# One order for all steps of a retention and SwiGLU kernel is replaced by another

## The chip, the cores and the metric

The kernel runs on one core of a Trainium2 chip (trn2). The time is that of one execution on the device in microseconds (us), the median of several executions.

## The reference

A retention layer (a linear attention with a decay per head) feeds a SwiGLU feed-forward block. All data is fp32.

```python
batch, n_heads, seq, head_dim = (4, 8, 768, 64)
for t in range(S):
    state = gamma * state + k_t (outer) v_t          # one 64 x 64 state per batch and head
    y[:, :, t] = scale * (q_t @ state)
x = y as (3072 tokens, 512)
g = x @ w_gate                                       # 512 x 1536
out = (g * sigmoid(g) * (x @ w_val)) @ w_out         # 1536 x 512
```

## The kernel before

**The work.** The 3072 tokens are cut into four segments of 768 tokens, numbered 0 to 3. A segment is six chunks of 128 tokens: three pairs (p = 0, 1, 2), the two of a pair from two batches. A segment has three stages: attention (its output y becomes the input x of the block), up (12 tiles f of the hidden width, gate and value), and down (12 tiles f, six token groups per tile). fp32 accuracy comes from three terms: each matrix is split into three parts, and every product is three matmul passes a = 0, 1, 2 over these parts. The three parts of an operand are made by three steps on three engines in turn: ScalarE (part 0), VectorE or GpSimd (part 1), GpSimd or VectorE (part 2).

**Stages in time.** Segment 0 loads the weights from the inputs in raw form, converts them and stores them in DRAM for the later segments. The attention of segment s+1 runs inside the down stage of segment s: its small matmuls stand between the down matmuls. So the order in time is: attention of segment 0 (the head), up 0, down 0 with attention 1, up 1, down 1 with attention 2, up 2, down 2 with attention 3, up 3, down 3. The up stages of segments 1 to 3 use seven products instead of eight (`up3`), which needs sums of x and of the weights.

**The order.** Each step is a small function with a key. `PLAN` is one string with all 2371 keys. `run()` walks it and calls each step; a call issues all instructions of the step, each on its engine or DMA queue. Every engine, and the SyncE queue that issues nearly all DMAs, executes in the order of issue. So `PLAN` fixes the order on each of them. Semaphores between engines are set by the framework from what each instruction reads and writes. Buffers of the splits rotate (four `gitem`, three `oitem`), and the PSUM banks are named in the code.

```python
    def run():
        for key in PLAN.split():
            if key in events:
                events.pop(key)[2]()
            else:
                do(key)
```

**Keys of segment 0.** `ln:w` loads chunk n (w = 0 k turned, 1 q turned, 2 v, 3 k by rows; DMA L472). The q of chunks 0 and 1 are loaded on ScalarE's queue ahead of `PLAN`. `A0 A1 A2` load the table of decays in three parts (two masks, and the rest; L594). `U`, `V` load raw weights (L519). `sn` is the scores of chunk n (PE L636, then two VectorE multiplications by the masks, L642), `kn`/`Kn` the scaled keys (GpSimd or VectorE L657), `tn` the state (PE L692), `on` the part of the old state (PE L707), `mn` the output (PE L721, then ScalarE L977), `xn:1`, `xn:2` the other two parts of x. `a b S c C` convert raw weights, `T` makes sums of weights in the buffer `first` (VectorE L407), `Z` stores these to DRAM (L490). `n` splits weights, `p`, `v` (PE L914) and `G`, `W` (PE L896) are the gate and value products.

**Keys with a segment, `s/...`.** `D f.tok` are three down matmuls (PE L1128). `h f.0` to `h f.2` split the hidden tile (ScalarE L968, VectorE L971, VectorE L407); `d f.0` to `d f.2` split `w_out` in segment 0 (ScalarE L977, GpSimd L980, VectorE L984); `W f` loads it. Attention of pair p: `sc p` the scores, `A p`, `B p`, `C p` the three groups of PE passes (all PE L766, 64x64 matmuls), `dec`, `q`, `k` the scalings, `was p.z` the decayed state (ScalarE L865), `new p.z` two adds of the new state out of PSUM (VectorE L871), `y p.z j` eight copies of y out of PSUM (ScalarE L999) for each half z, `sum`, `x` the sums and splits of x. Banks 6 and 7 hold all that `A`, `B` and `C` write, and `new` and `y` read. `w`, `p`, `u` are weights, products and the SwiGLU arithmetic of `up3`, `L` loads a tile of up weights, `e` writes out.

**One buffer twice.** `first` (segment 0: chunk 5's q and k, three sums of weights, one raw w_out tile) and `xb` (a part of x from segment 1 on) have the same place in SBUF. The first write to `xb` is `1/x0.2.0` on ScalarE; the last store out of `first` is `Z10`.

Of the kernel before, what the change touches and what calls it, by code (L numbers as in the profile page):

```python
# [25 lines left out]
L = 3  # L26
# [30 lines left out]
    p1:1 x5:2 Z0 u1:1 T1:2 c12 v1:0 U5:1 y1:0 v1:1 p0:2 Z1 l5:3 v0:2 c2 C2 b12 y1:1 p1:2 n2:0 a4
    U6:0 u0:2 b3 n2:1 u1:2 v1:2 S12 n2:3 L y0:2 S3 c3 n2:2 U13:2 G2:0 i2:0 n2:4 y1:2 C3 g4 T2:0
    b4 T2:1 n3:0 C12 n2:5 G2:1 i2:1 a5 T2:2 n3:1 Z2 n3:2 S4 n3:3 n3:4 c4 T3:0 C4 W2:0 j2:0 T3:1
    W2:1 G3:1 U7:1 c13 T3:2 G3:0 n4:0 Z12 n3:5 n4:1 i3:1 W3:0 Z3 n4:2 b5 a6 j2:1 i3:0 S5 n4:3  # L60
    G4:1 n4:4 c5 W3:1 T4:0 h2 U8:0 C5 T4:1 T4:2 n4:5 G4:0 a13 i4:1 n5:0 j3:0 n5:1 n5:3 n5:2 b6
    U14:3 i4:0 a7 W4:0 n5:4 j3:1 G5:1 S6 c6 b13 Z4 j4:0 T5:0 T5:1 C6 W4:1 n6:0 U9:1 T5:2 n5:5 b7
    a8 S13 W5:0 G5:0 j4:1 c14 Z5 W5:1 i5:0 i5:1 n6:1 S7 j5:1 n6:3 n6:4 c7 a9 C7 n7:0 n6:2 G6:0
    U10:0 j5:0 b8 G6:1 T6:0 n7:1 n7:3 S8 C13 T6:1 i6:1 i6:0 n6:5 n7:2 c8 Z13 l4:3 a14 n7:4 b14
    W6:1 W6:0 T6:2 C8 T7:0 S14 U15:2 n7:5 n8:0 j6:0 G7:1 j6:1 i7:1 U11:1 C14 b9 G7:0 n8:3 W7:1
    S9 n8:1 c15 n8:2 W7:0 c9 Z6 i7:0 j7:1 a10 P1 C9 n8:4 G8:1 n8:5 T7:1 j7:0 n9:0 b10 Z14 k4
    U16:3 g5 T7:2 S10 T8:0 G8:0 n9:1 a15 b15 P2 c10 Z7 W8:0 T8:1 n9:2 S15 T8:2 Z8 W8:1 C15 C10
    n9:3 i8:1 i8:0 k5 G9:1 Z15 a11 b11 j8:0 j8:1 n10:0 n9:4 S11 n9:5 t4 U17:2 c16 n10:1 G9:0
    T9:0 i9:0 t5 n10:3 n10:2 W9:1 a16 b16 n10:4 n10:5 S16 W9:0 T9:1 j9:0 P0 i9:1 c11 0/h0.0
    G10:0 G10:1 C11 n11:0 j9:1 W10:1 n11:3 i10:0 C16 Z16 i10:1 T9:2 n11:4 Z9 T11:0 T11:1 n11:5  # L70
    a17 b17 T11:2 W10:0 n11:1 T10:0 Z11 0/h0.1 S17 T10:1 j10:0 0/W0 c17 0/h1.0 n11:2 h1 G11:0
    C17 j10:1 i11:0 0/d0.0 G11:1 1/sc0 1/dec0.0 0/W1 1/l3 1/l5 1/q0.0 i11:1 0/h2.0 0/d0.1 0/h0.2
    0/h4.0 0/d1.0 W11:0 0/d0.2 1/k0.0 W11:1 1/l4 j11:0 0/D0.0 0/D0.2 1/dec0.1 0/d1.1 j11:1
# [14 lines left out]
    1/sc2 0/D6.3 1/sum1.2 0/D7.2 1/x1.2.1 1/sum1.1 0/h9.1 1/dec2.0 0/D7.4 0/Z7 1/q2.0 0/D7.0  # L88
    1/q2.1 0/D7.5 0/h10.0 1/dec2.1 0/d8.0 0/h10.1 0/W9 1/k2.0 0/D7.3 1/k2.1 1/sum1.3 1/x1.0.0
    0/D7.1 1/A2 0/d8.1 0/d8.2 0/d9.0 1/L0 1/x1.1.2 1/x1.1.1 1/new2.0 0/D8.4 0/d9.1 0/h11.0  # L90
    0/D8.2 0/h9.2 0/d9.2 0/D8.1 0/D8.0 1/x1.2.2 0/D8.5 0/W10 0/h11.1 0/h11.2 0/Z8 0/d10.0
    0/d10.1 0/D9.4 1/B2 0/d10.2 0/D8.3 1/y2.00 0/h10.2 1/w0.0.0 1/y2.01 1/y2.06 0/W11 1/y2.02
    0/D9.0 1/w0.0.1 0/D9.1 1/y2.07 0/D9.2 0/D9.3 1/y2.03 1/y2.04 1/y2.05 1/C2 0/D9.5 1/y2.16
    0/D10.0 1/y2.15 1/L1 1/x1.0.1 0/D10.3 0/Z9 1/y2.11 0/D10.1 1/x1.0.2 1/w0.0.2 1/y2.14 0/d11.0
    1/y2.17 0/D10.2 1/y2.13 1/sum2.0 1/y2.10 0/d11.1 0/d11.2 1/y2.12 0/Z10 0/D10.4 1/x2.1.0
    0/D10.5 1/sum2.1 1/w0.1.0 1/sum2.3 1/L2 0/D11.3 1/sum2.2 0/D11.4 0/D11.1 1/x2.0.0 1/x2.1.2
    0/D11.0 1/w1.0.0 0/D11.2 1/x2.1.1 1/x2.0.1 0/D11.5 1/x2.2.0 1/w1.0.1 0/e0 1/p0.0 0/Z11
    1/x2.0.2 1/u0.0 1/w1.0.2 1/p0.1 1/p0.2 1/u0.1 1/x2.2.1 1/p1.0 1/p1.1 0/e2 1/w0.1.1 1/w0.2.0
# [1205 lines left out]
```

## Time and profile before

| | |
|---|---|
| median of 3 executions | 648.29 us (647.54 to 648.67) |
| the profiled execution | 652.34 us |
| span of its instructions | 650.5 us |
| PE busy | 635.7 us |
| VectorE busy | 489.6 us |
| ScalarE busy | 392.4 us |
| GpSimd busy | 272.3 us |
| moved by DMA | 140.13 MB |

A profile row gives the start of an instruction or a merged group, its length, engine, source line, operation, output and inputs, shape and count; in brackets stands how long the engine was idle before, and what ended that. PE is TensorE's matmul part, PEld its weight load, DVE VectorE, ACT ScalarE, POOL GpSimd, SPq the queue of SyncE. PEclk is the share of the full TensorE clock that was granted. An fp32 matmul of 64 rows, and any other that isn't split by hand, shows as two.

### The profile page before, as it was taken

The page shows a single profiled execution, that of the slowest core. Times are in us where ns is not written, and L with a number is a line of the kernel's source. Part 1 is how long each engine was busy: PE and PEld are TensorE (multiplying, and loading weights), DVE is VectorE, ACT ScalarE, POOL GpSimd, SP SyncE. Part 2 cuts the span into 40 slices and gives each one's busy share as a digit, 9 for nine tenths or more (in the row PEclk, how much of TensorE's full clock was granted, in tenths as well). Part 3 has the DMA queues.
Part 4 walks back from the last instruction along what each step waited for, and adds up shares of the span by engine and source line. Part 5 has one row for each costly group of instructions (what it writes and reads, how often), then busy time and mean ns, then how long its engine had stood idle before and what let it go on. Part 6 is the DMA issues. An engine that isn't in the chain of part 4 may idle for free.

```text
span 650.5 us, 14090 instructions
## 1 busy us (share of the span) xinstructions
PE 635.7 (98%) x5576; PEld 581.5 (89%) x5576; DVE 489.6 (75%) x712; ACT 392.4 (60%) x860; POOL 272.3 (42%) x174
## 2 busy tenths in 40 slices
...
GB/s 323 374 356 332 350 327 278 198 361 261 300 183 313 152 146 171 36 245 248 247 215 209 235 116 65 123 194 286 115 260 270 156 188 141 133 11 158 177 215 147
DMA packets 50050, 140.13 MB, mean 215 GB/s; under 512 B 4928, under 2 KB 17472, under 8 KB 49984
## 3 DMA queue, kind: packets, MB, share of 16 engines
...
## 4 chain that ended last, share of the span: by engine, by line
PE 89%; DMA 4%; DVE 3%; ACT 2%; issue 1%; SPq 0%; ACTq 0%; DVEq 0%
PE bank L1065 40%; PE bank L1128 27%; PE bank L896 13%; PE bank L766 5%; PE bank L914 2%; DMA rawp<-in_w_gate_dram 1%; ACT chunk_x L999 1%; DMA hT<-in_k_n_dram 1%; DMA hT<-in_q_t_dram 1%; DVE oitem L984 0%; DMA loads<-in_v_n_dram 0%; DVE xb L407 0%; PE bank L721 0%; ACT states L865 0%; DVE tmp L407 0%
## 5 line engine op out<-in xcount | busy, mean ns | idle before, releaser
L1128 PE MATMUL bank<-oitem,gitem 128*128 128x512 f32 x864 | 210.9, 398 | 5.6 <-DVE oitem L984 2.9
L1128 PEld LDWEIGHTS bank<-oitem,gitem 128*128 128x128 f32 x864 | 160.5, 189 | 41.8 <-DVE oitem L984 4.4
L974 POOL TENSOR_TENSOR gitem<-gitem 128x768 fp32r<-128x768 f32 x72 | 143.7, 2005 | 100.7 <-DVE gitem L971 74.2
L1065 PE MATMUL bank<-xa,gitem 128*128 128x384 f32 x864 | 160.7, 334 | 0.0
L1065 PEld LDWEIGHTS bank<-xa,gitem 128*128 128x128 f32 x864 | 150.8, 188 | 0.3 <-ACT tmp L1081 0.2
L974 POOL TENSOR_TENSOR oitem<-oitem 128x256 fp32r<-128x256 f32 (+1 forms) x60 | 67.7, 1132 | 70.1 <-DVE oitem L971 56.1
L971 DVE SCALAR_TENSOR_TENSOR gitem<-gitem,loads 128x768 fp32r<-128x768 f32 x72 | 81.1, 1143 | 7.5 <-ACT gitem L968 5.8
L1065 PE MATMUL bank<-xb,gitem 128*128 128x384 f32 x432 | 85.2, 335 | 0.0
L896 PE MATMUL bank<-xa,oitem 128*128 128x384 f32 x480 | 84.2, 335 | 0.0
L896 PEld LDWEIGHTS bank<-xa,oitem 128*128 128x128 f32 x480 | 83.0, 188 | 0.2
L968 ACT ACTIVATE gitem<-loads 128x768 fp32r<-128x768 f32 x72 | 59.2, 842 | 31.8 <-PE bank L1065 24.4
L1065 PEld LDWEIGHTS bank<-xb,gitem 128*128 128x128 f32 x432 | 76.0, 188 | 0.7 <-POOL gitem L974 0.3
L971 DVE SCALAR_TENSOR_TENSOR gitem<-gitem,hT 128x768 fp32r<-128x768 f32 x48 | 50.3, 1053 | 30.1 <-ACT gitem L968 30.0
L968 ACT ACTIVATE gitem<-hT 128x768 fp32r<-128x768 f32 x48 | 40.0, 840 | 41.1 <-PE bank L1128 37.5
L999 ACT COPY chunk_x<-bank 64x128 f32<-64x128 f32 x144 | 35.5, 260 | 33.2 <-PE bank L766 28.4
L793 POOL TENSOR_TENSOR loads<-loads,tab 128x512 f32<-128x512 f32 x9 | 13.7, 1517 | 98.6 <-PE bank L766 83.1
L407 DVE SCALAR_TENSOR_TENSOR gitem<-gitem 128x768 fp32r<-128x768 f32 x48 | 45.9, 962 | 1.1
L1065 PE MATMUL bank<-xb,oitem 128*128 128x384 f32 x216 | 43.6, 336 | 0.0
L1065 PEld LDWEIGHTS bank<-xb,oitem 128*128 128x128 f32 x216 | 37.9, 188 | 0.2
L971 DVE SCALAR_TENSOR_TENSOR oitem<-oitem,loads 128x256 fp32r<-128x256 f32 (+1 forms) x42 | 32.5, 780 | 2.3 <-ACT oitem L968 2.2
L1080 ACT COPY tmp<-bank 128x384 f32<-128x384 f32 x36 | 17.2, 478 | 25.6 <-PE bank L1065 21.4
L980 POOL TENSOR_TENSOR oitem<-oitem 128x512 fp32r<-128x512 f32 x12 | 20.4, 1697 | 27.7 <-ACT oitem L977 27.7
...
## 6 DMA issues: line engine op xcount, KB each, us to landing
loads<-wup SPq DMA_DIRECT2D x36, 896.0 KB, 4.8
...
wup<-first SPq DMA_DIRECT2D x9, 896.0 KB, 5.7
...
```

The source lines that it names most:

```text
L407: stt(o, x, 1.0, y, op0=mul, op1=op)
L766: nc.tensor.matmul(o, a, b, start=start, stop=True, skip_group_check=True)
L793: (pool if i else both)(t, t, qdec, op=mul)
L896: nc.tensor.matmul(o, w[:, a, ts(b, P)], X0[:, a, i, NC - 1 - b], start=a == b == 0, stop=a == 2 and b == NC - 1, skip_group_check=True)
L968: act(o[0], x, AF.Copy, scale=CUT / FAR)
L971: stt(o[1], f32(o[0]), -FAR, x, op0=mul, op1=add)
L974: op(o[2], f32(o[0]), f32(o[1]), op=add)
L980: op(o[1], f32(o[0]), x, op=sub)
L999: copy(cx[half[i], ds(2 * h, 2), c, half[z]], y.rearrange("p (b t) -> p b t", b=2))
L1065: nc.tensor.matmul(o, w[:, a, k], x[:, a, KH - 1 - k], start=start and a == k == 0, stop=a == 2 and k == KH - 1, skip_group_check=True)
L1080: steps = (lambda: copy(p1, x), lambda: tt(c11, z, p1, op=add), lambda: act(gate, c11, AF.Silu, scale=ONE), lambda: copy(u2, x), lambda: c ...
L1128: nc.tensor.matmul(banks[tok], hs[f][:, a, ds(i * TH + u * P, P)], wo[f][:, a], start=f == a == 0, stop=f == NF - 1 and a == 2, skip_group ...
```

## The change

`PLAN` is replaced by another order of the same 2371 keys. No function, instruction, buffer or bank changes; the buffers of the splits are taken in the same order. Most keys move by a few places; the order on every engine and on the DMA queue changes in many places. The stores out of `first` stand ahead of the writes to `xb`, as they did before. What is written here is the head, and the stretches in the down stage of segment 0 that hold the attention of pairs 0 and 1 of segment 1.

```diff
 PLAN = """
-    l0:0 l1:0 A0 A1 s0 U0:0 l0:2 l0:3 a0:1 s1 b0:1 A2 h0 S0:1 m0 K0 x0:2 c0:1 l2:0 x0:1 l2:1
-    l1:3 C0:1 t0 l1:2 V0:0 l3:1 n0:0 s2 a0:0 Q2 l3:0 l2:3 n0:1 b0:0 S0:0 m1 k1 x1:1 x1:2 l2:2
-    c0:0 n0:2 U1:1 C0:0 t1 o2 l3:3 g2 s3 n0:3 n0:4 l4:1 p0:0 m2 a1:1 x2:1 k2 q3 b1:1 l4:0 a1:0
-    x2:2 S1:1 l5:1 l3:2 n0:5 c1:1 k3 t2 C1:1 o3 b1:0 l5:0 l4:2 g3 v0:0 s4 S1:0 t3 l5:2 c1:0 C1:0
...
-    0/h1.1 0/D0.1 0/d1.2 0/W2 1/q0.1 0/D0.4 1/k0.1 1/was0.0 0/D0.5 0/Z0 0/h1.2 0/h2.1 0/D0.3
-    T10:2 0/d2.0 Z17 0/h3.0 1/A0 1/new0.0 0/D1.0 0/h3.1 0/Z1 0/d2.1 0/D1.4 1/B0 1/y0.01 0/h4.1
-    0/W3 1/y0.05 Z10 1/y0.06 1/y0.03 1/y0.00 1/y0.02 1/y0.04 0/D1.3 0/d2.2 1/begin 1/y0.07
-    0/D1.1 1/was0.1 0/h2.2 0/d3.0 0/D1.5 0/h4.2 0/D1.2 1/C0 1/y0.12 1/y0.15 1/y0.11 1/y0.14 0/Z2
-    0/d3.1 1/y0.10 0/h3.2 1/y0.17 1/y0.16 0/D2.3 1/y0.13 1/x0.2.0 0/D2.2 1/new0.1 0/d3.2 0/D2.4
...
-    0/W4 1/sum0.0 0/D2.1 1/sum0.1 1/x0.2.1 0/D2.0 0/D2.5 1/x0.1.0 1/l7 0/Z3 0/h5.0 1/sum0.3
-    1/x0.1.1 0/d4.0 0/d4.1 1/x0.1.2 1/sc1 1/dec1.1 0/D3.2 1/q1.1 1/sum0.2 1/l6 1/dec1.0 0/D3.4
-    1/q1.0 0/D3.1 0/W5 0/D3.3 0/d4.2 0/h5.1 1/was1.0 1/k1.1 0/D3.5 0/D4.4 1/k1.0 0/D3.0 0/D4.3
-    0/h6.0 1/A1 1/l8 0/d5.0 1/x0.2.2 0/D4.2 1/l9 0/D4.5 0/W6 0/d5.1 0/h5.2 0/h6.1 1/x0.0.0
...
-    0/d6.1 1/was1.1 1/x0.0.2 1/C1 0/d7.0 0/h7.1 0/h7.2 1/y1.17 0/Z5 0/d6.2 1/l11 0/D6.2 0/D6.0
-    0/D5.5 1/y1.10 1/y1.15 0/h8.1 1/y1.11 1/y1.16 0/d7.1 1/y1.14 1/y1.12 1/y1.13 1/x1.2.0 0/Z6
-    1/new1.1 0/h8.2 1/x1.1.0 1/sum1.0 0/D6.1 0/h9.0 0/d7.2 0/D6.4 1/was2.0 0/W8 0/D6.5 1/l10
...
+    l1:0 A2 l0:0 A1 A0 l0:2 U0:0 l2:1 l0:3 s0 a0:1 l2:0 s1 m0 K0 b0:1 V0:0 S0:1 c0:1 l1:2 x0:2 s2
+    l1:3 l3:0 x0:1 C0:1 l3:1 k1 U1:1 l2:3 t0 l2:2 l4:0 a0:0 g2 n0:0 Q2 l4:1 n0:1 m1 b0:0 S0:0 c0:0
+    n0:2 t1 x1:1 a1:1 l3:3 x1:2 o2 C0:0 a1:0 s3 b1:1 S1:1 l3:2 q3 l5:1 n0:3 n0:4 c1:1 p0:0 l5:2 k2
+    l5:0 o3 C1:1 m2 n0:5 t2 s4 b1:0 k3 v0:0 x2:2 S1:0 u0:0 g3 l4:2 U2:0 c1:0 m3 n1:0 U12:3 x2:1 t3
...
+    0/D0.4 1/k0.1 1/l5 0/D0.0 0/h2.1 0/d1.2 0/h1.2 0/h4.0 0/W2 0/Z0 1/A0 1/y0.06 1/new0.0 0/h4.1
+    1/y0.01 0/D0.5 0/D0.3 0/d2.0 1/B0 0/D1.1 0/h3.0 1/y0.03 0/D1.5 1/y0.04 0/Z1 1/y0.02 1/y0.07
+    1/y0.05 T10:1 1/was0.1 1/y0.15 1/y0.00 1/y0.14 0/d2.1 0/D1.4 1/y0.12 0/d2.2 0/D1.2 1/y0.13 0/W3
+    Z17 0/D1.3 0/Z2 0/d3.0 0/D1.0 0/h2.2 0/h3.1 1/C0 0/W4 T10:2 0/h3.2 0/d3.1 0/h4.2 Z10 1/y0.16
+    1/l7 1/y0.17 1/new0.1 1/sum0.0 0/D2.3 0/D2.1 1/y0.10 0/h5.0 1/begin 1/sum0.1 0/d3.2 0/h5.1
+    1/y0.11 0/D2.5 1/sc1 0/D2.0 0/d4.0 1/was1.0 0/D2.4 0/d4.1 0/D3.4 1/l6 1/dec1.1 0/h5.2 1/dec1.0
+    0/D2.2 1/x0.2.0 0/D3.1 1/q1.1 0/d4.2 0/W5 0/D3.5 1/x0.1.0 0/h6.0 1/k1.0 0/Z3 1/sum0.3 1/k1.1
+    1/sum0.2 1/x0.2.1 0/D4.5 0/D3.2 0/D3.3 0/D3.0 1/q1.0 0/Z4 0/h6.1 0/D4.0 0/D4.4 1/x0.1.2 1/x0.1.1
...
+    1/was1.1 0/D5.5 1/C1 0/d7.0 1/y1.16 0/d7.1 0/D6.5 0/D5.0 1/y1.17 1/y1.15 1/new1.1 0/h7.2 1/y1.14
+    1/y1.11 0/D5.1 1/y1.13 1/x1.2.0 0/D6.3 0/d7.2 0/D6.4 0/Z6 1/y1.10 0/D7.3 0/h9.0 1/sc2 0/h8.2
...
```

More of the change, by code (lines that the diff above doesn't have):

```diff
@@ L57 @@
[L57 to L73, printed above, removed]
-    0/h1.1 0/D0.1 0/d1.2 0/W2 1/q0.1 0/D0.4 1/k0.1 1/was0.0 0/D0.5 0/Z0 0/h1.2 0/h2.1 0/D0.3
@@ L87 @@
-    1/new1.1 0/h8.2 1/x1.1.0 1/sum1.0 0/D6.1 0/h9.0 0/d7.2 0/D6.4 1/was2.0 0/W8 0/D6.5 1/l10
[L88 to L98, printed above, removed]
@@ L129 @@
-    1/D2.2 1/D2.0 1/D2.1 2/l11 2/y0.05 2/y0.06 1/h4.1 2/y0.02 2/y0.01 2/y0.00 2/y0.04 1/D2.3
-    1/D2.4 1/h3.1 2/was0.1 2/y0.03 1/h3.2 3/begin 1/W3 2/C0 2/new0.1 1/h5.0 1/D2.5 1/D3.4 1/D3.5
-    2/y0.11 1/D3.2 2/y0.13 2/y0.17 2/l5 2/y0.14 2/y0.15 2/y0.16 1/D3.1 2/y0.10 1/W4 1/h4.2
-    1/D3.3 2/sum0.0 1/D4.3 2/l7 2/x0.2.0 1/h5.1 1/h6.0 1/h6.1 1/h6.2 1/D4.2 2/y0.12 1/D3.0
-    1/D4.4 2/x0.2.1 2/l6 1/D4.1 1/h5.2 2/sc1 2/q1.0 2/dec1.0 2/x0.1.0 1/D4.0 2/sum0.1 1/W5
-    2/k2.1 2/dec1.1 2/was1.0 1/W6 2/k1.0 1/D4.5 2/x0.1.2 1/h7.0 1/h7.1 1/D5.1 1/D5.4 1/D5.5
@@ L135 @@
-    2/k2.0 2/sum0.2 2/k1.1 2/x0.2.2 1/D5.2 1/W7 2/q1.1 2/sum0.3 1/D5.0 2/A1 1/D6.0 1/D6.1
-    2/x0.0.0 2/new1.0 2/x0.1.1 2/B1 1/h8.0 1/D5.3 1/D6.4 2/y1.01 1/h7.2 2/y1.05 2/y1.03 2/l9
-    2/y1.07 2/y1.06 2/l8 1/D6.5 2/y1.00 2/x0.0.2 2/y1.02 2/y1.04 1/h9.0 1/D7.1 2/x0.0.1 2/was1.1
-    2/C1 1/D7.0 2/y1.16 1/h8.1 2/y1.17 1/W8 1/h8.2 2/y1.12 1/h9.1 2/new1.1 2/y1.14 2/y1.15
-    2/y1.13 1/D6.2 1/D6.3 1/D7.4 2/y1.10 2/y1.11 2/sc2 2/l10 2/sum1.0 2/x1.2.0 2/sum1.1 1/D8.1
-    1/h10.0 2/sum1.2 1/D7.5 2/L0 2/x1.1.0 2/dec2.1 2/dec2.0 1/D7.3 1/D7.2 2/sum1.3 2/q2.0 2/q2.1
@@ L183 @@
-    3/y0.15 3/x0.2.0 3/l6 2/D4.5 3/y0.13 3/x0.1.0 2/D4.1 3/was1.0 3/sum0.0 2/D4.0 3/sc1 3/x0.2.2
-    2/D5.4 2/h6.2 2/D5.5 2/D5.1 2/D5.0 3/k1.1 3/x0.1.2 2/W6 2/h7.0 2/D5.3 3/k1.0 3/q1.0 3/sum0.1
-    3/q1.1 3/x0.1.1 3/dec1.1 3/dec1.0 3/sum0.3 3/sum0.2 2/D5.2 3/A1 2/h8.0 2/W7 3/x0.0.0 2/D6.2
-    2/h7.1 2/W8 2/h9.0 3/new1.0 2/D6.1 3/x0.2.1 3/x0.0.2 3/B1 3/y1.01 2/D6.0 3/y1.04 2/h7.2
-    3/y1.03 3/x0.0.1 3/y1.07 2/h8.1 3/l8 3/y1.02 3/y1.00 3/y1.06 2/D6.4 2/D7.2 2/h8.2 3/y1.05
-    2/D6.5 3/C1 3/was1.1 3/y1.14 3/y1.17 2/D6.3 3/new1.1 3/y1.15 3/y1.16 2/D7.1 3/sum1.0 3/y1.12
@@ new lines @@
+    1/D2.2 2/y0.05 1/h4.1 3/begin 2/was0.1 2/C0 2/l5 1/D3.3 2/y0.16 1/h5.0 1/D3.5 1/D3.0 2/y0.17
+    2/new0.1 2/y0.11 2/k2.0 1/W4 1/D2.4 1/h4.2 2/x0.2.0 1/D3.4 2/l7 2/y0.13 1/D4.5 1/D3.2 2/y0.10
+    2/k2.1 2/sum0.0 1/D3.1 1/h6.0 1/h5.1 2/sum0.1 2/sc1 2/x0.1.0 2/was1.0 2/k1.1 1/D4.2 1/h6.1
+    2/x0.2.2 1/D4.0 1/D4.1 2/k1.0 2/x0.2.1 1/W5 2/sum0.2 2/dec1.0 1/h5.2 1/D5.1 1/D4.3 1/D5.5
+    2/dec1.1 1/h6.2 2/x0.1.1 2/q1.1 1/D4.4 2/q1.0 2/l6 1/W6 2/A1 1/D5.4 1/h7.0 1/h7.1 2/sum0.3 1/W7
+    2/new1.0 2/x0.0.0 2/x0.1.2 1/D5.0 1/D5.2 2/B1 1/D6.0 1/h8.0 1/h7.2 2/y1.02 2/y1.00 2/l9 2/y1.05
```

280 lines of the change are left out of this document (157 added, 123 removed).

## The prediction

> **What bounds the kernel now.** I read the page first, then the busy times by stage, then what PE waited for.
>
> ```profile
> PE 635.7 (98%) x5576; PEld 581.5 (89%) x5576; DVE 489.6 (75%) x712; ACT 392.4 (60%) x860; POOL 272.3 (42%) x174
> ```
>
> PE is busy for 635.7 of 650.5 us. An order can win at most the 14.8 us between. Where they lie is told by the stages (start and end in us; busy time and count by engine; granted clock, DMA share, GB/s):
>
> ```profile
> 0.00:4.95 4.95, 3.78 (x16) 3.49 (x17) 0.19 (x1) 1.49 (x2) 0.20 (x4) 1.00 0.55 187
> 4.95:32.00 27.05, 23.01 (x345) 20.58 (x346) 21.62 (x37) 15.30 (x31) 9.39 (x8) 1.00 1.07 378
> 32.00:127.00 95.00, 95.00 (x608) 94.28 (x608) 78.50 (x118) 77.31 (x116) 46.67 (x30) 1.00 0.88 311
> 127.00:200.00 73.00, 70.11 (x980) 55.88 (x979) 66.87 (x88) 50.61 (x144) 30.98 (x18) 1.00 0.81 281
> 283.00:352.00 69.00, 68.70 (x979) 55.79 (x978) 50.89 (x80) 46.63 (x140) 9.70 (x6) 1.00 0.70 243
> 437.00:510.00 73.00, 70.30 (x973) 56.53 (x972) 52.72 (x80) 46.74 (x138) 10.26 (x6) 0.95 0.70 230
> ```
>
> After the head (until 32) PE has no gap until 127. In down 0 it loses 73.00 - 70.11 = 2.89 us, in down 1 0.30, in down 2 2.70. Down 0 is also the only stage where VectorE is nearly full (66.87 of 73). These gaps, one by one:
>
> ```profile
> PE bank L1128 <- DVE oitem L984: 2.9, 2, 1.7
> PE bank L1128 <- issue: 2.7, 1, 2.7
> 156.22 1.88 PE L1128 MATMUL bank<-oitem,gitem 128*128 128x512 f32 x7 [1.69 <-DVE oitem L984]
> 185.18 0.49 PE L1128 MATMUL bank<-oitem,gitem 128*128 128x512 f32 x1 [1.20 <-DVE oitem L984]
> 458.31 1.01 PE L1128 MATMUL bank<-oitem,gitem 128*128 128x512 f32 x2 [2.70 <-issue]
> 455.60:458.30 2.70, 0.01 (x1) 0.00 (x0) 0.00 (x0) 2.63 (x10) 0.00 (x0) 0.85 0.09 27
> 458.30:464.30 6.00, 5.99 (x59) 4.44 (x58) 0.00 (x0) 0.07 (x1) 0.00 (x0) 0.50 0.01 3
> ```
>
> The two gaps of down 0 wait for VectorE's last part of a w_out tile (`0/d4.2`, `0/d9.2`). The gap at 455.6 waits for nothing that the profile names, and for 6 us behind it the clock is 0.50: together it costs about 2.70 + 6.00 x 0.5 = 5.7 us. The profiled execution took 652.34 us (span 650.5 and 1.84 around it); the median of the three executions is 648.29, 4.05 less. No other loss of that size stands in the trace, so I take it that the timed executions mostly lack this stall. I sum changes against the profiled execution and carry them over to the median.
>
> **Down 0: what the new order removes.** VectorE is late because it stands idle twice:
>
> ```profile
> 144.40 0.65 PE L766 MATMUL bank<-loads 64*64 64x64 f32 x32
> 145.23 1.96 ACT L999 COPY chunk_x<-bank 64x128 f32<-64x128 f32 x8
> 147.22 0.75 DVE L871 TENSOR_TENSOR states<-states,bank 128x256 f32<-128x256 f32 x2 [2.34 <-ACT chunk_x L999]
> 168.25 2.06 ACT L999 COPY chunk_x<-bank 64x128 f32<-64x128 f32 x8
> 170.34 0.75 DVE L871 TENSOR_TENSOR states<-states,bank 128x256 f32<-128x256 f32 x2 [1.86 <-ACT chunk_x L999]
> ```
>
> The add `1/new0.1` needs the passes of `1/C0`, which end at 145.05, yet it starts at 147.22, when the eighth copy `1/y0.1j` is done. It doesn't use their output. So users of one PSUM bank on two engines go in the order of issue, also where both only read. In the old `PLAN` all eight copies stand ahead of the add. In the new one `y0.12` to `y0.15` stand ahead of `C0`, then `y0.16`, `y0.17`, the add, and the last two behind it. After `C0` two copies of 1.96 / 8 = 0.25 us are left: the add can start at 145.05 + 0.5 = 145.6, 1.6 us earlier. For `1/new1.1` four of eight remain ahead of it, one before `C1`, three behind: 168.25 + 3 x 0.26 = 169.0, 1.3 us earlier. Together VectorE gets 2.9 us.
>
> Behind that add the order changes too:
>
> ```profile
> 155.49 0.68 DVE L984 SCALAR_TENSOR_TENSOR oitem<-oitem 128x512 fp32r<-128x512 f32 x1
> 183.36 1.76 DVE L984 SCALAR_TENSOR_TENSOR oitem<-oitem 128x512 fp32r<-128x512 f32 x1
> ```
>
> The first row is `0/d4.2`: it comes 8.3 us after the add starts. In the new order only `sum0.0`, `sum0.1`, `d3.2`, `h5.1`, `h5.2`, `dec1.1`, `dec1.0` (and the add) lie between, all of 0.4 to 1.0 us, some 5.5 us. It would be ready at about 151.8, and PE, whose first step with it (`D4.5`) now comes a little earlier, needs it near 153: the 1.69 us go. What is late next is its own input: `W4` now issues behind `Z17` and `Z2`, and the ScalarE and GpSimd steps follow its landing; I see 1 to 2 us of room. The second row is `0/d9.2`. Its place among VectorE's work stays, but the 2.9 us lie ahead of it, and the first PE step that uses it comes 1.9 us of PE work later (`B2`, `D8.5` go first). Its 1.20 us go too if VectorE's other work isn't stretched; this row itself took 1.76 us where the same operation took 0.68. So of 2.89 us I count 2.6; the bounds are 0.5 (VectorE stays the limit) and 2.9.
>
> **The stores out of `first`.**
>
> ```profile
> 139.20 0.74 DVE L871 TENSOR_TENSOR states<-states,bank 128x256 f32<-128x256 f32 x2
> 139.86 1.82 DVE L971 SCALAR_TENSOR_TENSOR gitem<-gitem,hT 128x768 fp32r<-128x768 f32 x2
> 139.30 0.32 SPq L490 DMA_DIRECT2D wup<-first  x1
> wup<-first SPq DMA_DIRECT2D x1, 896.0 KB, 5.8
> 147.22 0.94 ACT L977 ACTIVATE xb<-chunk_x 128x256 fp32r<-128x256 f32 x2
> ```
>
> `Z10` (third row) issues when `T10:2` ends and lands 5.8 us later, at 145.1; the first write to `xb` is at 147.22. The old order has this covered, so the named part alone wins nothing. In the new one VectorE does `new0.0`, `h4.1`, `d2.2`, `h2.2`, `h3.1` ahead of `T10:2`, about 4 us (first two rows and their like), and SyncE stands at `W4` until `D1.0` is done: `Z10` issues near 144 and lands near 150. ScalarE now does `h5.0`, `d4.0`, `was1.0` (2.7 us) ahead of the write and comes to it near 150. I cost it at nothing; uncovered, ScalarE and the splits behind stand for up to 1 us, inside the 0.5 bound above.
>
> **The head.**
>
> ```profile
> 4.95 2.98 PE L636 MATMUL bank<-hT 64*128 64x128 f32 x32
> 9.81 1.09 PE L721 MATMUL bank<-tmp,hT 128*64 128x128 f32 x16 [1.89 <-DMA hT<-in_v_n_dram]
> 13.21 1.04 POOL L657 TENSOR_TENSOR hT<-hT,tab 128x512 f32<-128x512 f32 x1 [12.76 <-DMA hT<-in_k_n_dram]
> 14.72 0.64 PE L692 MATMUL bank<-hT 128*64 128x64 f32 x16
> 15.65 1.09 PE L707 MATMUL bank<-loads,states 64*64 64x128 f32 x16 [0.30 <-DVE loads L651]
> 24.06 1.16 PE L636 MATMUL bank<-hT 64*128 64x128 f32 x16 [0.47 <-DMA hT<-in_k_t_dram]
> 25.51 0.69 PE L692 MATMUL bank<-hT 128*64 128x64 f32 x16 [0.29 <-DVE first L561]
> 27.00 1.16 PE L636 MATMUL bank<-first 64*128 64x128 f32 x16
> ```
>
> DMA is full here (378 GB/s in the stage row): 256 KB cost 0.69 us. `l0:0` drops from the first to the third place on SyncE, so `s0` starts up to 1.4 us later; the 1.89 us gap before `m0` mostly takes that. The load that hurts is `l1:3`: 768 KB more stand ahead of it (`V0:0` with 512 and `l1:2` with 256 now go first), 3 x 0.69 = 2.1 us. `k1` on GpSimd (13.21) moves to 15.3, ends at 16.35, and `t1` starts at 16.4 and not at 14.72: 1.7 us. Behind it PE has the same steps up to `m5`, with gaps of 0.30 + 0.47 + 0.29 = 1.06 us that can take up some: 0.6 to 1.7 us stay. The last loads, `l5:0` and `l4:2`, each have one more 256 KB ahead, so `s5` (27.00) can't start much earlier. With new small waits for the splits of the first product the worst I find is 2.1. I take 1.0, bounds 0.2 and 2.1. PE has no gap from there to 127, so all of it reaches the end.
>
> By the Trainium skill, "TensorE: Matmul & The Clock Gate", What's actually happening, the array runs at half clock until one busy window of about 3.4 us has passed, and the pause of `s0` behind the warm-up matmuls would put that off. The rows agree that the first two score steps are slow (2.98 us, against 1.16 for one later).
>
> **The other stages.**
>
> ```profile
> 328.69 1.26 PE L766 MATMUL bank<-loads 64*64 64x64 f32 x64 [0.30 <-ACT chunk_x L999]
> ```
>
> The up stages keep almost the same order. In down 1 the 0.30 us at `2/sc2` waits for a copy of y that now stands earlier: -0.3. Against it PE steps in down 1 and 2 move up to 2 us earlier against their VectorE and ScalarE inputs, whose room was often near 1 us. I take +0.3, bounds 0 and 1.3. The DMA queue keeps its loads within a place or two there; the `W` loads go ahead of the `l` loads (`W5` before `2/l6`), which helps.
>
> **The sum.** -2.6 (down 0), +1.0 (head), -0.3, +0.3: -1.6 us. From 652.34 that is 650.7 with the stall at 455.6, and from the median 648.29 - 1.6 = **646.7 us**. What a measurement of this kernel can tell from no change is about 0.2%, 1.3 us.
>
> **The rivals.** *PE waits for copies (slower).* The new order puts copies ahead of later PE passes on the same banks, in some ten places (`y0.06`, `y0.01` ahead of `1/B0`, four copies ahead of `1/C0`, `y1.12` ahead of `1/C1`, the same in pairs of segments 2 and 3).
>
> ```profile
> 138.50 1.66 PE L1128 MATMUL bank<-oitem,gitem 128*128 128x512 f32 x6
> ```
>
> Between `A0` and `B0` PE has two down steps, 1.66 us, and in that time a copy (0.26), the two adds (0.74) and a copy (0.26) must follow one another: 1.26 us and their hand-overs. From some 0.3 us of delay on VectorE or ScalarE on, PE waits. At 0.5 us in each of ten places that is +5: 646.7 + 5 = 651.7. For it speaks that VectorE is 92% busy in down 0; against it that it is near 72% in down 1 and 2, and most places have more than 0.3. *VectorE stays the limit of down 0*, through stretched rows like the 1.76: only 0.4 us go, 646.7 + 2.2 = 648.9. *Slow clock in the head*: the pause makes `s1` and `m0` run as slowly as `s0`, 2.98 - 2 x 1.16 = 0.7 us or a little more: 647.5. That is the time by the Trainium skill's rule above. *The stall of 455.6 moves*: if one comes into the timed executions, 646.7 + 5.7 = 652.4; if a rest of it leaves them, some 1.5 less, 645.2.
>
> **How the numbers follow.** Forecast 0.46, of which 0.34 lie over 0.2% below the median and 0.12 within; copies 0.25 (slower); VectorE 0.10 and slow clock 0.07 (both within); the stall 0.12, half faster, half slower. So faster 0.40, same 0.29, slower 0.31. The range goes from 644.6 (the best bounds, -2.9 + 0.2 - 0.3 + 0 = -3.0, and some of the stall's rest) to 651.8, which takes in the copies at their price. The forecast's own range is 645.3 to 648.
>
> **What would show it.** Right: no gap at `0/D4` and `0/D9` in down 0, VectorE's wait before `1/new0.1` at 0.7 us or less and before `1/new1.1` at 0.6 or less; `t1` near 16.4; the first steady stretch of PE about 1.0 us later than 31.88. Wrong: gaps of PE at `B` or `C` passes released by ScalarE copies or VectorE adds, ScalarE idle before its first `xb` write, a head over 2 us longer, or another gap with no releaser.

## The result and the profile after

The new order takes 644.40 us (median of 6 executions, 643.75 to 645.73), the old one on the same chip 648.13 (6 executions, 647.54 to 648.67). The ratio is 0.9943, its 95% interval 0.9930 to 0.9956: 3.7 us faster. The forecast was 646.7 with a range from 644.6 to 651.8. The direction is right, the size 2.3 us short, and the result lies just below the range.

In the kernel files of this part the lines lie 8 or 9 lower than in the kernel before (`PLAN` is wrapped into fewer lines): L1120 and L1119 are the down steps (L1128 before), L1057/L1056 the up steps, L758/L757 the attention passes, L976/L975 the last part of a w_out tile.

First the page of after, its row of busy time, then the stages in the stretches used before (start and end in us; busy time and count of PE, PEld, DVE, ACT, POOL; granted clock, DMA share, GB/s):

```profile
PE 632.8 (99%) x5576; PEld 580.2 (90%) x5576; DVE 487.8 (76%) x712; ACT 391.8 (61%) x860; POOL 264.5 (41%) x174
```

```profile
4.95:32.00 27.05, 22.73 (x334) 20.58 (x336) 21.38 (x35) 14.43 (x32) 10.35 (x9) 1.00 1.06 376
127.00:200.00 73.00, 72.98 (x999) 59.26 (x998) 68.94 (x91) 52.57 (x145) 31.39 (x19) 1.00 0.87 305
283.00:352.00 69.00, 69.00 (x979) 55.74 (x978) 52.06 (x80) 48.05 (x141) 9.85 (x6) 1.00 0.72 239
437.00:510.00 73.00, 72.98 (x947) 59.99 (x943) 58.80 (x84) 48.86 (x139) 15.31 (x9) 1.00 0.69 230
```

PE has no idle time left in any of the three down stages (2.89, 0.30 and 2.70 us before). All that PE still waits for stands in this answer (us in total, times, longest), and all of it lies in the head:

```profile
PE bank L628 <- DMA hT<-in_k_t_dram: 3.3, 2, 1.8
PE bank L1209 <- DVE warm L1224: 1.1, 1, 1.1
PE bank L684 <- POOL hT L649: 0.8, 1, 0.8
PE bank L713 <- DMA hT<-in_v_n_dram: 0.3, 1, 0.3
```

The first steady matmul of PE (`p0:1`) in before and in after, from the two timelines:

```profile
31.88 1.34 PE L914 MATMUL bank<-xa,oitem 128*128 128x256 f32 x9
```

```profile
32.73 1.46 PE L906 MATMUL bank<-xa,oitem 128*128 128x256 f32 x10
```

So the profiled executions are nearly accounted for. The span fell from 650.5 to 642.1, by 8.4: head +0.85, down 0 -2.87, `2/sc2` -0.30, the stall at 455.6 -2.70, and half of the 6.00 us of matmuls at a clock of 0.50 behind it, -3.0. (The clock record shows 0.50 for 6.83 us, but PE still stands in the first 0.83 of them.) That adds up to -8.0; the other 0.4 us stand in no gap. The timed executions won only 3.7 us. Without the stall's 5.7 us the sum would be -2.3, so some 1.4 us of what the timed executions won is not in the gaps that name a releaser. Where that comes from is the question of the experiments.

### The profile page after: what moved, and what is told of

Read it like the earlier page. It is cut to its first block, busy times and chain, and to the rows that moved or that the text cites. A ratio compares the mean times of both kernels' runs of the same rounds, so it can differ in the third digit from the quotient of the medians.

```text
span 642.1 us, 14098 instructions
## 1 busy us (share of the span) xinstructions
PE 632.8 (99%) x5576; PEld 580.2 (90%) x5576; DVE 487.8 (76%) x712; ACT 391.8 (61%) x860; POOL 264.5 (41%) x174
## 4 chain that ended last, share of the span: by engine, by line
PE 97%; DMA 2%; SPq 0%; POOL 0%; ACT 0%; issue 0%; POOLq 0%
PE bank L1057 41%; PE bank L1120 32%; PE bank L888 13%; PE bank L758 6%; PE bank L906 3%; DMA hT<-in_k_n_dram 1%; DMA tab<-in_decays_dram 1%; PE bank L713 1%; PE bank L699 1%; PE bank L628 1%; PE bank L684 0%; POOL hT L649 0%; SPq L586 0%; SPq L464 0%; ACT chunk_x L1142 0%
## 5 line engine op out<-in xcount | busy, mean ns | idle before, releaser
L1120 PE MATMUL bank<-oitem,gitem 128*128 128x512 f32 x864 | 208.5, 395 | 0.0
L1120 PEld LDWEIGHTS bank<-oitem,gitem 128*128 128x128 f32 x864 | 159.0, 188 | 35.3 <-DMA oitem<-wdnt 0.5
L966 POOL TENSOR_TENSOR gitem<-gitem 128x768 fp32r<-128x768 f32 x72 | 140.6, 1963 | 116.6 <-DVE gitem L963 98.6
L1057 PE MATMUL bank<-xa,gitem 128*128 128x384 f32 x864 | 160.5, 334 | 0.0
L1057 PEld LDWEIGHTS bank<-xa,gitem 128*128 128x128 f32 x864 | 150.8, 188 | 0.2
L966 POOL TENSOR_TENSOR oitem<-oitem 128x256 fp32r<-128x256 f32 (+1 forms) x60 | 65.7, 1102 | 53.0 <-DVE oitem L963 51.2
L1057 PE MATMUL bank<-xb,gitem 128*128 128x384 f32 x432 | 84.5, 334 | 0.0
L963 DVE SCALAR_TENSOR_TENSOR gitem<-gitem,loads 128x768 fp32r<-128x768 f32 x72 | 75.1, 1058 | 9.2 <-ACT gitem L960 7.8
L1057 PEld LDWEIGHTS bank<-xb,gitem 128*128 128x128 f32 x432 | 75.9, 188 | 0.4
L963 DVE SCALAR_TENSOR_TENSOR gitem<-gitem,hT 128x768 fp32r<-128x768 f32 x48 | 46.2, 965 | 25.4 <-ACT gitem L960 25.4
L399 DVE SCALAR_TENSOR_TENSOR gitem<-gitem 128x768 fp32r<-128x768 f32 x48 | 49.1, 1030 | 0.8
L1057 PE MATMUL bank<-xb,oitem 128*128 128x384 f32 x216 | 43.4, 335 | 0.0
L1057 PEld LDWEIGHTS bank<-xb,oitem 128*128 128x128 f32 x216 | 38.0, 188 | 0.3
L1074 DVE TENSOR_TENSOR hT<-bank,tmp 128x384 f32<-128x384 f32 x36 | 20.0, 554 | 20.1 <-PE bank L1057 19.9
L963 DVE SCALAR_TENSOR_TENSOR oitem<-oitem,loads 128x256 fp32r<-128x256 f32 (+1 forms) x42 | 34.1, 816 | 0.9 <-ACT oitem L960 0.8
```

Of the source, the lines that this page charges most:

```text
L399: stt(o, x, 1.0, y, op0=mul, op1=op)
L963: stt(o[1], f32(o[0]), -FAR, x, op0=mul, op1=add)
L966: op(o[2], f32(o[0]), f32(o[1]), op=add)
L1057: nc.tensor.matmul(o, w[:, a, k], x[:, a, KH - 1 - k], start=start and a == k == 0, stop=a == 2 and k == KH - 1, skip_group_check=True)
L1074: lambda: copy(p5, wb), lambda: tt(h1, x, p5, op=add),
L1120: nc.tensor.matmul(banks[tok], hs[f][:, a, ds(i * TH + u * P, P)], wo[f][:, a], start=f == a == 0, stop=f == NF - 1 and a == 2, skip_group ...
```

## The experiments

All but two of these kernels reorder `PLAN` alone; the two repeat the old and the new order unchanged. A list cut in pieces keeps each piece's own order, and steps already issued are left out of the next piece. Times are compared with the kernel before on the same chip: its median was 649.32 beside the four kernels of the first part, 648.83 beside `adds_first`, `adds_last`, `l11_first` and `head_old`, and 649.37 beside the last four.

**The old order again, and the stages one by one.**

```
b_again:    PLAN of before
head_new:   PLAN of after up to p0:1, the rest in before's order
down0_new:  before up to 1/sc0, after up to 1/p0.0, the rest as before
down2_new:  before up to 3/sc0, after up to 3/p0.0, the rest as before
```

> The kernel before, unchanged, profiled and timed once more. Its first profiled execution took 652.34 us with a stall of 2.70 us at 455.6 us and half clock for 6.83 us behind it (6.1 us in all); without them it would have been 646.2, yet the timed executions of before have a median of 648.13. Theory A (the timed executions hold a rest of the stall): a second profile again has a wait of PE with no releaser in a down stage, of some other length, with the mean clock below 1.00 when it is long; span between 645 and 650.5. Theory B (the stall was a single event and the timed executions differ by something the profile of before shows elsewhere): a second profile has no such wait, and a span near 646.4 (648.1 - 1.8) with other gaps than the first: the head or down 0 longer by 1.4 to 1.9 us.

Measured: 648.41 against 649.32, ratio 0.9992 (0.9982 to 1.0002). What PE waited for in this profile (four of its rows), and the timeline at the stall:

```profile
PE bank L712 <- DMA hT<-in_v_n_dram: 3.2, 1, 3.2
PE bank L1119 <- DVE oitem L975: 2.9, 2, 1.7
PE bank L1119 <- issue: 0.5, 1, 0.5
PE bank L757 <- POOL tmp L789: 0.5, 1, 0.5
```

```profile
457.29 1.08 PE L1119 MATMUL bank<-oitem,gitem 128*128 128x512 f32 x4 [0.53 <-issue]
```

The wait that names no releaser is back, 0.53 us long where it was 2.70, ahead of the same matmul: inside `2/D2.5`. The two down-0 gaps are back to a tenth (2.9). A fourth loss is one that the first profile lacks: `3/A2` waits 0.52 us for GpSimd's `3/k2.0`. Probably the long stall and the slow clock had given GpSimd the time; no run tests that. The span is 647.6 all the same, because the head was longer: `p0:1` starts at 33.23 us, `m0` having waited 3.2 us for its v load and the clock record showing 0.50 for 6.83 us behind that. Theory A holds; B's longer head is there too. (The 6.1 us of the expectation count the 0.83 us of half clock in which PE stands anyway; 5.7 is the cost.)

> The new order up to the first steady matmul of PE (p0:1), the old order for all behind. The two profiles show p0:1 start at 32.73 us in after against 31.88 in before. If that is what the new head costs: +0.85 us in the time (649.0). If the missing 1.4 us of the prediction lies in the head of the timed executions: -0.5 us (647.6). The head's own gaps: s0 starts near 6.67 behind l0:0, s1 near 1.78 us long, t1 near 16.8.

Measured: ratio 1.0011 (0.9999 to 1.0024), +0.7 us (-0.1 to +1.6). That agrees with +0.85 and speaks against a gain in the head. `p0:1` started at 33.41 here. The stall was there, again in `2/D2.5`, and the first wait of down 0 too:

```profile
PE bank L1119 <- DVE oitem L975: 2.9, 2, 1.6
PE bank L1119 <- issue: 1.2, 1, 1.2
```

> The old order up to the first score pass of down 0 (1/sc0), the new one up to the first step behind down 0 (1/p0.0), the old one again behind. If the two gaps of PE at 0/D4 and 0/D9 are what the new order wins: -2.9 us (645.2), with no wait of PE for VectorE in down 0. If more of the change lies in down 0 than the profile shows: -4 or less (644.1). If the new order there depends on the new order before it (the stores Z10 and Z17): -1 or nothing, with new gaps.

Measured: ratio 0.9964 (0.9953 to 0.9975), -2.3 us (-3.1 to -1.6). No wait of PE for VectorE's w_out parts is left. Part of the third case is there too: a new gap of 1.03 us stands ahead of the first down step, by the profile a wait for a scaling on ScalarE, and after doesn't have it. So the new order of down 0 seems to need a little of the new order ahead of it. The stall in the old down 2 is still there (0.76 us in `2/D2.5`):

```profile
PE bank L1119 <- ACT loads L792: 1.0, 1, 1.0
455.44 0.84 PE L1119 MATMUL bank<-oitem,gitem 128*128 128x512 f32 x3 [0.76 <-issue]
```

> The old order, with the new one only from the first score pass of down 2 (3/sc0) to the first step behind it (3/p0.0). By the gaps that name a releaser the two orders are alike there: 0 us (648.1). If the timed executions of before lose 1.4 us in down 2 to the stall that names no releaser, and the new order doesn't: -1.4 us (646.7). A profile without the stall and the half clock would have a span near 644.4.

Measured: ratio 0.9973 (0.9960 to 0.9985), -1.8 us (-2.6 to -1.0). This is the missing part. With the new order in down 2 alone there is no wait that names no releaser; what is left in the stage is 0.94 us at `3/A1` for a v load:

```profile
437.00:510.00 73.00, 72.06 (x996) 58.96 (x996) 56.89 (x85) 47.92 (x140) 10.94 (x7) 1.00 0.73 240
```

```profile
PE bank L757 <- DMA loads<-in_v_n_dram: 0.9, 1, 0.9
```

The stages add up: -2.3 + 0.7 - 1.8 and the 0.3 at `2/sc2` give -3.7, each of the first three known to some 0.8 us.

**The bank order alone.** Each of the next two changes nothing but the places of the two adds and the copies around them.

```
adds_first, in before:
-  1/C0 1/y0.12 1/y0.15 1/y0.11 1/y0.14 0/Z2 0/d3.1 1/y0.10 0/h3.2 1/y0.17 ... 1/new0.1
+  1/C0 0/Z2 0/d3.1 0/h3.2 1/new0.1 1/y0.12 1/y0.15 1/y0.11 1/y0.14 1/y0.10 1/y0.17 ...
-  1/C1 0/d7.0 0/h7.1 0/h7.2 1/y1.17 ... 1/y1.10 1/y1.15 0/h8.1 1/y1.11 ... 1/new1.1
+  1/C1 0/d7.0 0/h7.1 0/h7.2 ... 0/h8.1 1/new1.1 1/y1.17 1/y1.10 1/y1.15 1/y1.11 ...
```

> The old order with the two adds 1/new0.1 and 1/new1.1 moved ahead of the copies of y that stood before them (behind 0/h3.2 and 0/h8.1). Theory A (users of one PSUM bank go in the order of issue, and the late adds alone make VectorE late for 0/d4.2 and 0/d9.2): VectorE starts the adds within 0.3 us of the end of 1/C0 and 0/h8.1 (2.1 and 1.8 us earlier), both gaps of PE in down 0 (1.7 and 1.2 us) go, -2.3 to -2.9 us, as much as the whole new order of down 0 gave (-2.3). Theory B (the earlier places of 0/d4.2 and 0/d9.2 in the new order are needed too): -1.0 us or less, with a gap left at 0/D9.

Measured: ratio 0.9950 (0.9933 to 0.9967), -3.2 us (-4.3 to -2.1), as much as the whole new order of down 0 or more. The add, and PE's waits for VectorE and for no named releaser:

```profile
144.89 0.75 DVE L862 TENSOR_TENSOR states<-states,bank 128x256 f32<-128x256 f32 x2 [0.25 <-PE bank L757]
```

```profile
PE bank L1119 <- DVE oitem L975: 0.4, 1, 0.4
PE bank L1119 <- issue: 1.2, 1, 1.2
```

The add now waits for the pass and not for copies. Of 2.9 us of gaps 0.4 is left. Two adds moved within one stage win what the gaps cost; the earlier place of `0/d4.2` isn't needed for it.

```
adds_last, in after:
-  1/y0.12 ... 1/y0.13 ... 1/C0 ... 0/h4.2 Z10 1/y0.16 1/l7 1/y0.17 1/new0.1 ... 1/y0.10 ... 1/y0.11
+  1/C0 ... 0/h4.2 1/y0.12 ... 1/y0.17 1/y0.10 1/y0.11 1/new0.1 Z10 1/l7 ...
-  1/y1.17 1/y1.15 1/new1.1 ... 1/y1.14 1/y1.11 ... 1/y1.13 ... 1/y1.10
+  1/y1.17 1/y1.15 1/y1.12 1/y1.14 1/y1.11 1/y1.13 1/y1.10 1/new1.1 ...
```

> The new order with only the bank order of 1/C0 and 1/C1 undone: all eight copies of y0.1 (y1.1: seven of eight) stand behind the pass and ahead of the add again. Theory A: 1/new0.1 starts some 2.2 us behind the end of 1/C0 (in after 0.03 and 0.55 for its two halves), 1/new1.1 some 2.2 us behind 1/C1; 0/d4.2, which in after is done only 0.2 us before PE needs it, becomes 1 to 1.6 us late: a gap of PE at the first 0/D4 step, +1.0 to +1.6 us against after (645.4 to 646.0 where after is 644.4). Theory B (the adds don't matter, the places of the w_out parts do): no gap, the time of after.

Measured: 648.19, ratio 0.9997 (0.9983 to 1.0012). The whole gain is gone. From the timelines of VectorE and PE, and PE's waits:

```profile
147.82 0.75 DVE L863 TENSOR_TENSOR states<-states,bank 128x256 f32<-128x256 f32 x2 [2.58 <-ACT chunk_x L991]
155.74 0.50 PE L1120 MATMUL bank<-oitem,gitem 128*128 128x512 f32 x1 [1.10 <-DVE oitem L976]
```

```profile
PE bank L1120 <- DVE oitem L976: 2.0, 2, 1.1
PE bank L758 <- DVE states L863: 0.4, 1, 0.4
```

VectorE stands 2.58 us behind eight copies. PE loses 1.10 us at `0/D4.5`, 0.86 at `0/D7.3` and 0.45 at `1/sc1`, which needs the bank that the add frees. That is 2.41 us and more than the 1.0 to 1.6 expected, since I had priced only the first. The profiled execution is 2.9 us above that of after (646.74 against 643.87), 0.5 more than these gaps. The timed ones are some 3.5 above it by the ratios; the difference of 0.6 lies within the interval.

**Why PE stands in 2/D2.5.** In every trace the instruction queue (q8 on the page) moves PE's program in 44 packets of 16 KB. In before and in the four kernels of the first part, wherever the stall is seen, PE goes on 1.3 to 1.5 us behind the end of packet 31 (counted from 0). So the theory is that PE waits for its own instructions; the three kernels below show the same 1.3 to 1.5 us wherever they stall. In the old down 2 the load `2/W4` issues 0.57 us ahead of the first matmul of `3/A0`, and `3/l11` follows it at once.

```
l11_first, in before:
-  2/W4 3/y0.12 2/D4.4 3/l11
+  3/l11 2/W4 3/y0.12 2/D4.4
w4_late, in before (W4 waits for the last D1 step):
-  2/D1.0 2/D2.3 3/A0 ... 2/D2.0 ... 2/D2.2
+  2/D2.2 2/D2.3 3/A0 ... 2/D1.0 ... 2/D2.0
w4_early, in after:
-  2/D2.2 ... 2/D1.3 ... 2/D1.4 ... 2/D2.3 ... 3/A0 2/D1.0
+  2/D1.3 ... 2/D1.4 ... 2/D1.0 ... 2/D2.3 ... 3/A0 2/D2.2
```

> The old order with one step moved: in down 2 the load 3/l11 (384 KB) goes ahead of the load 2/W4 on SyncE, as in the new order, so it issues near 447.3 us and not at 450.0. Theory A (the matmuls behind the third of 2/D2.5 wait for a block of instructions that is fetched late, because its packet stands behind W4 and l11 on the DMA engines; in the four profiles with the old down 2 it was fetched 3.6 to 5.5 us behind the first matmuls of 3/A0, in after 2 us): the block comes about 1 us earlier, the wait at 2/D2.5 (0.5 to 2.7 us) goes or stays under 0.3 us, time -0.6 to -1.2 us. Theory B (the wait comes from the order of PE's steps, one down step fewer between 3/A0 and 2/D2.5): wait and time as before (648 to 649).

Measured: ratio 1.0010 (0.9996 to 1.0024), no gain, and the stall was there:

```profile
PE bank L1119 <- issue: 1.6, 1, 1.6
```

Packet 31 started 4.4 us behind the first matmul of `3/A0`. The edit left the larger load, 768 KB of `W4`, where it was, so it can't tell the two theories apart; it shows that the place of `l11` alone isn't it.

> The old order with three steps of PE changed in place: 2/D2.2 ahead of 3/A0 and 2/D1.0, 2/D2.0 behind it, so the load 2/W4 (which waits for the last D1 step), and 3/l11 behind it on SyncE, issue behind 3/A0 (near 452) and not 0.6 us ahead of it; as many PE steps stand between 3/A0 and 2/D2.5 as before. Theory A (the late block of instructions stands behind 2/W4 on the DMA engines): the block is fetched about 2 us behind the first matmul of 3/A0 as in the new order, the wait at 2/D2.5 is under 0.3 us, time -0.8 to -1.5 us. Theory B (the fetch is late for another reason, one PE step fewer between 3/A0 and 2/D2.5 being what shows it): a wait of 0.5 us or more stays, time within 0.4 us of before.

Measured: ratio 0.9974 (0.9959 to 0.9989), -1.7 us (-2.7 to -0.7). There is no wait without a releaser. The stage, and then the DMA queues in the 3 us from the first matmul of `3/A0` on, in the first profile of before (450.2 to 453.2) and in w4_late (451.8 to 454.8; share of 16 engines at the end):

```profile
437.00:510.00 73.00, 72.47 (x998) 59.38 (x998) 55.19 (x85) 48.11 (x140) 15.35 (x7) 1.00 0.74 247
```

```profile
q1 hardware_dynamic: 204, 1.02, 100.1%
q14 instruction: 1, 0.01, 0.6%
```

```profile
q1 hardware_dynamic: 58, 0.26, 20.9%
q8 instruction: 1, 0.02, 2.0%
```

In before the data fill the engines and PE's packet doesn't come within the 3 us; in w4_late, where `W4` issues 2.33 us behind the first matmul of `3/A0`, it comes after 1.8. The 0.53 us that PE still loses in the stage are the wait of `3/A2` that `b_again` has too. (One of the gaps of down 0 was shorter in this profile, 0.07 us for 1.20, and one of 0.39 came further on, with nothing changed there. So the 1.7 us need not be the stall's alone.)

> The new order with 2/D1.3, 2/D1.4, 2/D1.0 ahead of 2/D2.3 and 3/A0, and 2/D2.2 behind 3/A0: 2/W4 issues some 0.7 us ahead of 3/A0, as in the old order, and not 2.3 us behind its start; the number of PE steps between 3/A0 and 2/D2.5 stays. Theory A: the block of instructions comes 1 to 2 us later than in after (there 1.9 us behind the first matmul of 3/A0), and a wait of 0 to 1 us appears at 2/D2.5, 0 to +1 us. Theory B: no wait, the time of after.

Measured: 646.51, ratio 0.9954 (0.9935 to 0.9973); after on the same chip took 644.51 (below). It is 2.0 us slower by the medians, more than the 0 to 1 expected. Its timeline and the same 3 us of the queues (447.2 to 450.2), and those of after (447.1 to 450.1):

```profile
453.72 0.21 PE L758 MATMUL bank<-loads,states 64*64 64x64 f32 x1 [1.07 <-issue]
```

```profile
q1 hardware_dynamic: 428, 0.91, 92.2%
```

```profile
q1 hardware_dynamic: 382, 0.65, 70.6%
q8 instruction: 1, 0.02, 2.6%
```

With `2/D1.0` ahead of `3/A0` and `2/D2.2` behind it, `W4` issues 0.58 us ahead of `3/A0` and not 2.32 us behind its start, and a stall of 1.07 us appears in an order that had none. Another 0.5 us is a wait of `3/A1` for a v load. Over all profiles the reading holds (times in us, the packet's from the first matmul of `3/A0` on):

```
kernel       packet 31 behind 3/A0   wait in 2/D2.5
before               5.6                 2.70
b_again              3.7                 0.53
head_new             4.3                 1.24
down0_new            3.4                 0.76
l11_first            4.4                 1.64
adds_first           3.9                 1.19
w4_early             4.0                 1.07 (at the end of 3/B0)
after, a_again, down2_new, adds_last, head_old, head_l13, w4_late   1.7 to 2.0   none
```

Two more figures of the traces speak for it. In all seven stalls PE stops at the same place of its program, behind 4162 matmuls in five traces and 4161 in two, whichever step stands there; so the wait belongs to a place in the program and not to a step or its data. And `W4` issues 0.57 or 0.58 us ahead of `3/A0` in all seven kernels that stall, and 2.32 or 2.33 us behind its first matmul in all seven that don't.

That the packet is late when `W4` issues ahead of `3/A0` is shown by two edits in opposite directions. How it stands behind the data is not: no trace has the time of its request, and full DMA engines alone don't decide it, for in `down2_new` data took 88.3% of the same 3 us and the packet was in time. By the Trainium skill, "DMA: Bandwidth & Descriptors", Queues, rings and completion order, an engine changes between its queues after each packet, which would let an instruction packet in early; the 3.4 to 5.6 us don't look like that, unless the request itself is late.

**The head, and after again.**

```
head_old:  PLAN of before up to p0:1, the rest in after's order
head_l13:  after, V0:0 moved behind l1:2 and l1:3
a_again:   PLAN of after
```

> The old head (up to p0:1) and the new order for all behind. If the new head costs what the stages showed (+0.7 us): 0.7 us faster than after, ratio to before 0.993 (-4.4 us). If the head's length is a matter of single executions (p0:1 started at 31.88, 33.23, 32.10 and 33.30 us with the old head, at 32.73 and 33.41 with the new): the time of after (ratio 0.9943).

Measured: 644.66, ratio 0.9939 (0.9921 to 0.9958). By its ratio that is the time of after: 0.7 us either way lies within the interval.

> The new order with one load moved in the head: V0:0 (512 KB) behind l1:2 and l1:3. If the head of after is set by l1:3, k1, t1 as the prediction has it: l1:3 lands 1.4 us earlier (near 14.2 us), t1 starts near 15.4 and not at 16.8, the first steady matmul (p0:1) up to 1.4 us earlier than 32.73; time -0.5 to -1.4 us against after. If t1's delay is taken up behind it (the old head had t1 at 14.7 to 16.8 and p0:1 at 31.9 to 33.3): the time of after within 0.3 us.

Measured: 644.45 against 644.51 for after in the same set. `l1:3` landed at 13.44 and not at 15.55, `t1` started 2.1 us earlier, and almost nothing came of it:

```profile
14.69 0.67 PE L684 MATMUL bank<-hT 128*64 128x64 f32 x16
16.75 1.09 PE L699 MATMUL bank<-loads,states 64*64 64x128 f32 x16 [1.39 <-DVE loads L643]
32.54 1.70 PE L906 MATMUL bank<-xa,oitem 128*128 128x256 f32 x12
```

The next step, `o2`, waits 1.39 us for VectorE, and `p0:1` starts at 32.54 where it was 32.73. The chain that ended last (start and length of each piece) no longer runs over `t1` here, but over a v load that lands at 21.93:

```profile
13.12 8.81 DMA hT<-in_v_n_dram
21.97 1.09 PE bank L713 x16
```

In after it runs from `l1:3` over `k1` to `t1`, and from there on PE has no gap up to `p0:1`:

```profile
8.06 7.49 DMA hT<-in_k_n_dram
15.69 1.05 POOL hT L649
16.79 0.69 PE bank L684 x16
```

So `t1` does set the end of the head in after, and the next limit stands 0.2 us behind it.

> The kernel after, unchanged, on the chip of the other three. Ratio to before 0.9943 as in its first runs (-3.7 us). Its second profile shows no wait of PE behind the head; a wait at 2/D2.5 would speak against the new order keeping the block of instructions in time.

Measured: 644.51, ratio 0.9919 (0.9900 to 0.9939). No stall, and no wait of PE behind the head. Its executions range over 1.8 us (643.49 to 645.27), those of before in that set over 4.2. No version tried beats after by more than the runs can tell.

## Why the prediction was wrong in size

**The step that failed is the stall at 455.6.** The prediction wrote that "the timed executions mostly lack this stall", because their median lay 4.05 us below the profiled one, and put it at nothing in the sum (only a rival of 0.06 allowed "some 1.5 less", and the lower end of the range took in 0.7 us of it). By their times, what the timed executions lack is its long form and the slow clock behind it. A wait of 0.5 to 2.7 us at the same matmul is in all six profiles of the old order of down 2, and the new order took it away: -1.8 us by `down2_new`. Put into the sum, -1.6 becomes -3.4, and 648.29 - 3.4 = 644.9, inside the range; the 0.5 us from there to 644.40 are within the interval (0.8 us either way). The cause that the reading missed is a load: in the new order `W4` issues behind `3/A0`, as two edits show. The prediction weighed SyncE's order in down 2 only for whether the data come in time.

**Down 0 was right, in mechanism and nearly in size.** -2.6 was forecast; the profile shows -2.87, `down0_new` -2.3 (-3.1 to -1.6). Users of one bank go in the order of issue, two readers too. After shows it for each bank by itself. These are the two halves of `1/new0.1` (first row; the second half waits until 146.49 for `1/y0.17`) beside the copies, and those of `1/new1.1`:

```profile
145.97 0.97 DVE L863 TENSOR_TENSOR states<-states,bank 128x256 f32<-128x256 f32 x2 [0.32 <-PE bank L758]
145.96 0.81 ACT L991 COPY chunk_x<-bank 64x128 f32<-64x128 f32 x3 [0.88 <-PE bank L758]
167.91 0.42 DVE L863 TENSOR_TENSOR states<-states,bank 128x256 f32<-128x256 f32 x1 [0.93 <-ACT chunk_x L991]
```

The first half starts beside a copy, because the copies still ahead of it read the other bank. VectorE waits 0.45 us at `new0.1` (0.7 or less was said) and 1.05 at `new1.1` (0.6 or less was said): there three copies and `1/was1.1` stand ahead. Ends compared with the pass, the adds come 1.9 and 1.0 us earlier, 2.9 in all as forecast. `0/d4.2`, however, was ready at 153.71 and not at 151.8, because two VectorE rows were stretched (`0/h5.2` to 2.1 us, and `0/d4.2` itself). PE's weight load for `0/D4.5` had to wait for it:

```profile
152.52 1.19 DVE L976 SCALAR_TENSOR_TENSOR oitem<-oitem 128x512 fp32r<-128x512 f32 x1
153.76 0.76 PEld L1120 LDWEIGHTS bank<-oitem,gitem 128*128 128x128 f32 x4 [0.20 <-DVE oitem L976]
```

The 0.20 us are hidden behind the matmuls that still run; the room that the prediction put at 1 us or more is used up.

**The head was right in chain and size.** +1.0 was forecast, the two profiles show +0.85, `head_new` +0.7 (-0.1 to +1.6). `l1:3` landed 2.5 us later (2.1 was said) and `t1` started at 16.79, 2.07 us later than in before (16.4 was said). Behind it before had gaps of 1.06 us and after has none: 2.07 - 1.06 = 1.0, near the 0.85. `head_l13` adds what the prediction did not see: a second limit stands 0.2 us behind this chain, so that an earlier `l1:3` alone wins next to nothing. And `head_old` doesn't show the 0.7 us in its time. A part is chance: with the old head `p0:1` started at 31.64 to 32.10 us in five profiles, and at 33.2 to 33.4 in the three in which `m0` had waited 3.0 us or more and the clock fell to 0.50 for 6.83 us.

**The small terms.** -0.3 at `2/sc2` came. The +0.3 for new small waits did not: PE waits for no copy and no add behind the head. `Z10` issued at 145.45 and landed at 151.32, ScalarE came to its first `xb` write at 151.43 after 0.45 us of waiting for it: later than said, hidden as said.

**The rivals.** Copies ahead of PE passes (+5): nothing of it in after; but `adds_last` shows one of the kind, 0.45 us at `1/sc1`. VectorE as the limit of down 0: no. Slow clock in the head: `s0` and `s1` took 3.63 us together in after against 2.98 before, about the 0.7 priced. But it cost nothing there, for PE then waits 1.52 us for the k load of `s2`, which would have been longer by as much:

```profile
6.67 3.63 PE L628 MATMUL bank<-hT 64*128 64x128 f32 x32 [1.80 <-DMA hT<-in_k_t_dram]
12.84 1.16 PE L628 MATMUL bank<-hT 64*128 64x128 f32 x16 [1.52 <-DMA hT<-in_k_t_dram]
```

The stall that leaves (645.2): this was the case, with 0.06 on it.
